# Third pair's preparation, the homes of the streamed factors and the order of masks in a fused routing-attention and feed-forward kernel

## The chip, the cores and the metric

The kernel runs on one core of one Trainium2 chip. A core has five engines with a queue of instructions each: TensorE (PE in the profile, with PEld for its weight loads), VectorE (DVE), ScalarE (ACT), GpSimd (POOL) and SyncE (SP), which here only issues transfers. The metric is the device time of one execution in microseconds (us); a kernel's time is the median of several executions.

## The reference

Attention with routing, then a feed-forward block. A query sees a key only if both fall to the same of 16 cluster centroids of their head.

```python
q_n, k_n, c_n = (t / (norm(t) + 1e-06) for t in (q, k, centroids))
q_assign = argmax(einsum('bhsd,hcd->bhsc', q_n, c_n), axis=-1)
k_assign = argmax(einsum('bhsd,hcd->bhsc', k_n, c_n), axis=-1)
mask = q_assign[:, :, :, None] == k_assign[:, :, None, :]
scores = where(mask, matmul(q, k.T) / sqrt(D), -1e9)
attn = softmax(scores)                      # (B, H, S, S)
x = matmul(attn, v)  ->  (B * S, H * D)
h = x @ w_in
out = (h - tanh(h)) @ w_out
```

The sizes are B = 4 batches, H = 8 heads, S = 768 positions, D = 64, a model width of 512 and an inner width of 2048. Inputs come as 64-bit floats, which the kernel reads as pairs of 32-bit words or rounds by itself; all matmuls are 32-bit.

## The kernel before

**Pairs, halves and steps.** Heads are taken in pairs: pair n is batch n // 4, heads 2p and 2p + 1 with p = n % 4; there are 16 pairs. A pair's 768 queries are two halves of 384, and its 768 keys are taken in three steps of 2 x 128. So one step is (pair, half, key step). The list `steps` starts with the first halves of pairs 0 to 3 (steps 0 to 11), goes on with their second halves (12 to 23), and then takes each later pair as a whole, six steps each (24 to 95). The number of a step is `at` in the code. `HP` is 4, `HALF` is 12, `NS` is 3, `HF` is 8, `CH` is 2.

**Work of one pair before its steps.** `load` fetches q, k and v (192 KB per head and input). `turn` transposes q and k so that D lies on the partitions: for pairs 0 to 3 by PE through a PSUM tile of the pool `ps_s` and a copy by ScalarE or VectorE. `similar` multiplies with the centroids into a PSUM tile of `ps_f`, `turn_back`, `route` and `route_on` find the cluster of each position on VectorE, `publish` writes the clusters of the queries as codes to DRAM, and `spread` reads them back, laid out to all partitions as a row (`row`); for the first half of pairs 1 to 3, `spread_both` fetches them into a tile `hot` instead, and `one_hot` makes from it two factors which PE adds to the scores, so that these steps need no mask on VectorE.

**Work of one step.** `begin` multiplies keys and queries (line 502, `sc`; with the factors of `hot`, line 513) and takes the exponential on ScalarE (line 524). `select` masks one of the step's two tiles on VectorE (line 534, two instructions, one for each head); after the second one GpSimd adds the tiles to a running sum (lines 546 and 550). `value` multiplies with v (line 559, `av`). The sums over keys are made by PE: in the first halves of pairs 0 to 3 in each step (`sum_up`, line 574, `den`), later from GpSimd's sums (`total_both`, line 620). In a turn of the step loop, PE is given the scores of the next step, the values of the current one, and then pieces of the feed-forward block as a fill; `todo` is the list of the other engines' work, the masks of the next step first, which is dealt out between the pieces of the fill (`between`).

**PSUM.** Scores and transposes share `ps_s` with two tiles; similarities, sums and the products of the feed-forward block share `ps_f` with three.

**The feed-forward block.** The first half of batch 0 is computed plainly (lines 733 and 749, steps 12 to 23). From step 24 on the products are made by a seven-product (Strassen-like) scheme: `up_product` (line 936, `pu`) for `x @ w_in`, `down_product` (line 1041, `pd`) for the second matmul. Its factors of w_in and w_out are sums of quarters, made once on VectorE (`up_maker` in steps 20 to 22, `down_maker` from step 36 on), kept in DRAM (`up_factors`, `down_factors`) and streamed back, 896 KB or 1024 KB at a time, by `fetch_factors`; three such tiles are held at once. `up_maker(0)` works on `w_in[0]` and `w_in[2]`, `up_maker(1)` on `w_in[1]` and `w_in[3]`. A streamed tile is asked for when product 6 of two before is made. `right_factors` makes differences of columns of x (`diff`, line 902), and the results of products are added on VectorE into `t`, `u`, `g` or `G` (line 931), which frees the PSUM tile. The plain and the first scheme's results go through tanh on ScalarE (line 990) and a subtraction on GpSimd (line 991).

**Weights.** w_in and w_out come in 32 pieces of 512 KB, which GpSimd asks for (`fetch`, three ahead), ScalarE works on twice (`rest_of`, lines 150 and 151) and VectorE twice (`round_piece`, lines 159 and 162); `paces` says how many in each step.

**What sets the order.** The kernel is emitted under a manual schedule: each engine runs its instructions in the order in which the code emits them, and waits on semaphores in that order. A transfer on SP waits in SP's queue until what it needs is there, and what stands behind it on SP waits too. The opening, before the loop over steps, is written out by hand:

```python
        load(1)
        load(0, (2,))
        turn(0, 0, nc.scalar); turn(0, 1, nc.vector)
        similar(0); turn_back(0); keep_warm(2); route(0); route_on(0)
        turn(1, 0, nc.scalar); turn(1, 1, nc.scalar); keep_warm(3)
        publish(0); load(2, (0,)); spread(0, 0)
```

`keep_warm(n)` gives PE n matmuls whose result nobody reads. The work of the pairs 2 and later before their steps is put into steps by the table `ready`; for pair 2 its transposes lie in step 0, its similarities and routing in step 1.

Of the kernel before, what the change touches and what calls it, by code (L numbers as in the profile page):

```python
# [58 lines left out]
def kernel(  # L59
# [120 lines left out]
    def fast():  # L180
# [18 lines left out]
        first_in = ExitStack()  # L199
        wp_in = first_in.enter_context(tc.tile_pool(name="wp_in", bufs=1, side="right"))  # L200
# [646 lines left out]
        def fetch_factors(n: int):  # L847

            if n < (B - 1) * PER:
                i = n + HF if n < 0 else n % PER  # L850
                t = streams[n] = late_pools["stream"].tile([P, HF, HM], F32, name="stream")
                if i < HF:
                    t = streams[n] = t.rearrange("p a b -> p (a b)")[:, 0 : 7 * CH * P].rearrange(
                        "p (c k f) -> p c k f", k=7, c=CH
                    )
                nc.sync.dma_start(t, up_factors[i] if i < HF else down_factors[i - HF])

        late_pools, half_pools, diffs = {}, {}, {}
        mid = ExitStack()

        def open_stream():
            first_in.close()
            late_pools["stream"] = cx.enter_context(
                tc.tile_pool(name="stream_late", bufs=3, side="right", reuse_waits="tile")
            )
            half_pools["diff"] = mid.enter_context(
                tc.tile_pool(name="diff_mid", bufs=1, side="right", reuse_waits="tile")
            )
            for n in range(2):
                fetch_factors(n - HF)  # L870

        def open_late():
            first.close()
            mid.close()
            for name, bufs in (
                ("diff", 1), ("u", 2), ("s", 2), ("th", 2), ("g", 1), ("left", 1), ("du", 1),
                ("c", 4), ("raw", 2), ("den", 1),
# [10 lines left out]

        def right_factors(b: int, c: int):

            if c == 0:
                diffs[b] = (
                    late_pools["diff"].tile([P, 3, CH, TB], F32, name="diff")
                    if b else half_pools["diff"].tile([P, 3, CH, TB // 2], F32, name="diff")
                )
# [99 lines left out]
        def strassen_items(b: int):  # L995
# [21 lines left out]
            def down_product(k_: int, j: int, between, rows_=False):  # L1017
# [25 lines left out]
                if which == 1:  # L1043
                    us[j] = late_pools["du"].tile([P, 2, HM], F32, name=f"du{j}")
# [74 lines left out]
        for n in range(2, len(pairs)):  # L1119
# [5 lines left out]
            for i, stage in enumerate(before(n)):  # L1125
                if stage:
# [60 lines left out]
        nc.gpsimd.tensor_copy(out=gate, in_=raw_qk[0, 1][:, 0, 1, 0:1])  # L1187
        for i in range(AHEAD):
            fetch(i)
        load(1)  # L1190
        load(0, (2,))
        turn(0, 0, nc.scalar)
        turn(0, 1, nc.vector)
        similar(0)
        turn_back(0)
        keep_warm(2)
# [4 lines left out]
        keep_warm(3)  # L1201
        publish(0)
        load(2, (0,))
        spread(0, 0)
        rest_of(0)
        similar(1)
        turn_back(1)
        keep_warm(1)
        load(2, (1,))
        rest_of(1)  # L1210

        nc.gpsimd.tensor_copy(out=gate, in_=rows[0, 0][:, 0, 0, 0:1])
        round_piece(rounding.pop(0))
        route(1)
        route_on(1)
        begin(steps[0])
        round_piece(rounding.pop(0))
        begin(steps[1])
        publish(1)
        select(*steps[0][:2], 0)  # L1220
        spread_both(1)
        begin(steps[2])
# [14 lines left out]
        paces = dict(enumerate((0, 0, 1, 1, 1, 0, 2, 1, 2, 1, 1, 0, 3, 2, 2, 2, 2, 2, 2, 3, 2)))  # L1237
# [3 lines left out]
        for at, (n, half, s) in enumerate(steps):  # L1241
# [4 lines left out]
            if at == 2 * HALF - 1:  # L1246
                open_stream()
# [3 lines left out]
            if at == 2 * HALF - 4:  # L1251
                makers = [it for i in range(2) for it in up_maker(i)]
            if at == 2 * HALF:
# [47 lines left out]
            if not taken:  # L1301
# [4 lines left out]
            if summed(n, half):  # L1306
                if 0 in stages:
                    stages.pop(0)()
                sum_up(n, half, s)
# [69 lines left out]
            if makers and at in light:  # L1379
                share = -(-len(makers) // len(light))  # L1380
                todo += makers[:share]
# [260 lines left out]
```

## Time and profile before

| what | us |
|---|---|
| median of 8 executions | 952.66 |
| lowest and highest of them | 950.91, 954.02 |
| the profiled execution | 953.53 |
| its span, first to last instruction | 951.8 |
| PE idle in the span | 17.2 |
| opening: first scores, first values | 15.43, 21.94 |
| scores of step 3 (first of pair 1) | 29.79 |
| first scores of step 25, with the fill of step 24 behind them | 195.57 |
| plain second matmul of batch 0's second half begins | 280.87 |

A line of a timeline has the start, the length, the engine, the line of the kernel, the operation with its tiles (written <- read) and shapes, the number of instructions, and in brackets the engine's idle time before it with what ended it. PE's records come two to a matmul of 32-bit numbers, so "x8" in the opening is four matmuls of the kernel. SPq, ACTq and POOLq are the queues that issue transfers; a line of theirs says when a transfer was issued, not when it landed. The chain that ended last follows the execution back from its last instruction; its shares say what the span was spent on.

### The profile page before, as it was taken

The numbers are of one execution on the slowest core, as the hardware profiler recorded it, in microseconds if no ns is written. First come the engines' busy times: TensorE is split into PE (matmuls) and PEld (weight loads), VectorE is DVE, ScalarE is ACT, GpSimd is POOL, SyncE is SP. The second block draws the span as 40 slices with busy tenths as digits, with TensorE's granted clock in tenths as the row PEclk, the third lists the DMA queues.
The fourth block names the chain that finished last, engine by engine and source line by source line (L and its number), as shares of the span: only waits on it lengthen the run. The fifth ranks groups of instructions, "written<-read, shape, count | busy, mean of one in ns | idle before, by whom it ended". The sixth has DMA issues, their size and how long they took to land.

```text
span 951.8 us, 16937 instructions
## 1 busy us (share of the span) xinstructions
PE 934.6 (98%) x6568; PEld 467.0 (49%) x6568; DVE 594.1 (62%) x1127; ACT 293.3 (31%) x453; POOL 510.7 (54%) x364
## 2 busy tenths in 40 slices
PE   8999999999999999999999999999999999999997
PEld 5434443355553334444466664444456665445664
DVE  7658677976687688657746567767756348443011
ACT  5586554223432232333321112332331220222000
POOL 1026343455665555778685453867797343657500
PEclk9999999999999999999999999999999999999999
DMA  8766454982737645474665646457344222323331
GB/s 201 199 193 145 156 139 128 277 248 74 191 102 185 158 129 125 154 188 108 193 166 195 153 144 204 114 177 181 113 130 148 98 84 101 117 80 131 107 106 37
DMA packets 168456, 139.92 MB, mean 147 GB/s; under 512 B 118272, under 2 KB 146736, under 8 KB 165680
## 3 DMA queue, kind: packets, MB, share of 16 engines
q1 hardware_dynamic: 161984, 117.23, 44.6%
q0 software_dynamic: 6240, 21.50, 6.7%
q8 instruction: 54, 0.88, 0.4%
q14 instruction: 34, 0.28, 0.1%
q10 hardware_dynamic: 144, 0.03, 0.0%
HBM read 117.48 MB, written 21.24 MB: 146 GB/s over the span
## 4 chain that ended last, share of the span: by engine, by line
PE 90%; DVE 5%; DMA 2%; POOL 1%; issue 1%; ACT 1%; SPq 0%; DVEq 0%; ACTq 0%; POOLq 0%
PE pu L936 25%; PE pd L1041 21%; PE sc L502 13%; PE av L559 13%; PE o L749 8%; PE h L733 4%; PE sim L378 1%; DVE e L534 1%; DMA stream<-up_factors 1%; PE den L574 1%; PE den L620 1%; POOL sum L550 1%; PE den L593 1%; DVE den L710 1%; DMA again<-in_moe_w_out_dram 1%
## 5 line engine op out<-in xcount | busy, mean ns | idle before, releaser
L550 POOL TENSOR_TENSOR sum<-sum,e 128x768 f32<-128x768 f32 x112 | 207.2, 1850 | 90.8 <-DVE e L534 86.0
L534 DVE SCALAR_TENSOR_TENSOR e<-row,code,sc 128x384 f32<-128x384 bf16 x336 | 186.0, 607 | 74.0 <-ACT sc L524 52.7
L1041 PE MATMUL pd<-stream,G 128*64 128x256 f32 (+1 forms) x1728 | 191.6, 379 | 0.0
L524 ACT ACTIVATE sc<-sc 128x768 f32<-128x768 f32 x168 | 125.9, 789 | 190.2 <-PE sc L502 156.6
L936 PE MATMUL pu<-xT,stream 128*64 128x384 f32 (+1 forms) x1024 | 159.3, 447 | 2.0 <-DVE g L931 0.9
L1041 PEld LDWEIGHTS pd<-stream,G 128*64 128x64 f32 (+1 forms) x1728 | 130.5, 144 | 61.7 <-issue 6.3
L502 PE MATMUL sc<-t,t 64*128 64x384 f32 x768 | 148.9, 506 | 0.5 <-ACT e L524 0.5
L559 PE MATMUL av<-e,vals 128*64 128x384 f32 x768 | 145.2, 498 | 1.2 <-DVE e L534 1.2
L1005 POOL TENSOR_TENSOR G<-G,th 128x768 f32<-128x768 f32 (+1 forms) x51 | 87.2, 1726 | 67.8 <-ACT th L1003 67.6
L936 PE MATMUL pu<-diff,stream 128*64 128x384 f32 (+1 forms) x768 | 120.8, 447 | 2.0 <-DVE G L931 1.0
L936 PEld LDWEIGHTS pu<-xT,stream 128*64 128x64 f32 x1024 | 73.1, 137 | 76.3 <-issue 60.0
L502 PEld LDWEIGHTS sc<-t,t 64*128 64x128 f32 x768 | 66.8, 186 | 73.6 <-issue 37.3
L546 POOL TENSOR_TENSOR sum<-e 128x768 f32<-128x768 f32 x28 | 52.7, 1881 | 74.4 <-DVE e L534 62.2
L559 PEld LDWEIGHTS av<-e,vals 128*64 128x64 f32 x768 | 47.5, 136 | 83.2 <-issue 77.9
L1003 ACT ACTIVATE th<-G 128x768 f32<-128x768 f32 (+1 forms) x51 | 40.9, 806 | 148.9 <-DVE G L931 144.1
L749 PE MATMUL o<-w_out,g 128*64 128x512 f32 x384 | 85.8, 592 | 0.0
L936 PEld LDWEIGHTS pu<-diff,stream 128*64 128x64 f32 x768 | 54.3, 137 | 59.4 <-issue 48.1
L931 DVE TENSOR_TENSOR G<-pu,u 128x384 f32<-128x384 f32 x72 | 39.7, 552 | 27.0 <-PE pu L936 27.0
L749 PEld LDWEIGHTS o<-w_out,g 128*64 128x64 f32 x384 | 27.5, 137 | 50.5 <-issue 50.0
L1056 DVE SCALAR_TENSOR_TENSOR c<-pd,du 128x256 f32<-128x256 f32 x36 | 15.1, 420 | 49.1 <-PE pd L1041 49.1
L733 PE MATMUL h<-xT,w_in 128*64 128x384 f32 x256 | 42.8, 486 | 0.0
L1056 DVE SCALAR_TENSOR_TENSOR du<-pd,du 128x256 f32<-128x256 f32 x31 | 13.0, 420 | 45.6 <-PE pd L1041 45.2
(139 smaller groups left out, 844.2 us busy)
## 6 DMA issues: line engine op xcount, KB each, us to landing
stream<-up_factors SPq DMA_DIRECT2D x32, 896.0 KB
stream<-down_factors SPq DMA_DIRECT2D x21, 1024.0 KB
raw<-in_moe_w_in_dram POOLq DMA_DIRECT2D x16, 512.0 KB, 4.5
raw<-in_moe_w_out_dram POOLq DMA_DIRECT2D x16, 512.0 KB, 4.6
again<-in_moe_w_in_dram SPq DMA_DIRECT2D x32, 256.0 KB
again<-in_moe_w_out_dram SPq DMA_DIRECT2D x32, 256.0 KB
vals<-in_v_dram SPq DMA_DIRECT2D x32, 192.0 KB
row<-q_codes SPq DMA_DIRECT2D x29, 192.0 KB
```

Of the source, the lines that this page charges most:

```text
L502: nc.tensor.matmul(sc[i][:, h, 0:TB], lhsT=turned[n, 1][r].rearrange("p a n -> p (a n)")[:, j * P : (j + 1) * P], rhs=turned[n, 0][r, half ...
L524: nc.scalar.activation(out=out, in_=sc[i][:, :, 0:TB], func=ACT.Exp, scale=SCALE)
L534: nc.vector.scalar_tensor_tensor(out=e[:, h].rearrange("p (j n) -> p j n", n=P), in0=rows[n, half][:, h], scalar=(codes[n][:, h, 1, j : j ...
L546: nc.gpsimd.tensor_tensor(out=s, in0=pair[0], in1=pair[1], op=ALU.add)
L550: nc.gpsimd.tensor_tensor(out=s, in0=s, in1=pair[i], op=ALU.add)
L559: nc.tensor.matmul(avs[n, half][h * D : h * D + D], lhsT=vals[n][:, h, j], rhs=e[i][:, h], start=(j == 0), stop=(j == NCH - 1),)
L733: nc.tensor.matmul(h[r], lhsT=w_in[i][:, c, o * P : (o + 1) * P][:, r], rhs=xT[c][:, half], start=(c == 0), stop=(c == CD - 1),)
L749: nc.tensor.matmul(acc[sub][r], lhsT=gs[f % HF][:, f // HF, sub * P : (sub + 1) * P][:, r], rhs=w_out[f // FQ][:, f % FQ], start=(f == seq ...
L936: nc.tensor.matmul(ps[r], lhsT=streams[base + i][:, c, k_, r], rhs=right[c], start=(c == 0), stop=(c == CH - 1),)
L1003: nc.scalar.activation(out=th, in_=t, func=ACT.Tanh)
L1005: nc.gpsimd.tensor_tensor(out=t, in0=t, in1=th, op=ALU.subtract)
L1041: nc.tensor.matmul(out_, lhsT=w, rhs=x, start=(i == 0), stop=(i == HF - 1))
```

## The change

Three parts, and what goes with them.

**The opening.** All of pair 2's q and k is loaded before the codes of pair 0 are published. Its transposes and similarities move from steps 0 and 1 ahead of the first values; its routing stays in step 1. The scores of steps 0, 1 and 2 are begun one by one as soon as their inputs exist. Five of the six filler matmuls between the pairs are gone. The first three weight pieces are no longer asked for together: each waits, through a copy on GpSimd into `gate`, for another transfer (pair 2's k, pair 0's row, pair 1's hot tile). The two pieces that were rounded in the opening are rounded in steps 1 and 5, and in a step of the first halves that has transposes these go ahead of the pieces on ScalarE.

**The factors.** Streamed factors no longer have tiles of their own in a pool that is opened in step 23 when w_in's is closed; they land in w_in[0], w_in[2] and w_in[1] in turn. The first two are asked for in step 21, once the first half of the factors has been issued, not in step 23. The differences of batch 0 and the scheme's `du` lie in w_in[3].

**The masks.** In steps 24 to 35 both masks of the next step are put ahead of the fill; before, the second one stood in slot 1 of the fill. Only in the step after a routing (26 and 32) both stand in slot 1. And in step 72, as in step 48 before, nothing is dealt out in the first piece of the fill.

```diff
@@ streams
-                t = streams[n] = late_pools["stream"].tile([P, HF, HM], F32, name="stream")
+                t = w_in[(0, 2, 1)[(n + HF) % 3]].rearrange("p c f -> p (c f)")
                 if i < HF:
-                    t = streams[n] = t.rearrange("p a b -> p (a b)")[:, 0 : 7 * CH * P].rearrange(
-                        "p (c k f) -> p c k f", k=7, c=CH
-                    )
+                    t = t[:, 0 : 7 * CH * P].rearrange("p (c k f) -> p c k f", k=7, c=CH)
+                else:
+                    t = t[:, 0 : HF * HM].rearrange("p (a b) -> p a b", b=HM)
+                streams[n] = t
                 nc.sync.dma_start(t, up_factors[i] if i < HF else down_factors[i - HF])
...
-        def open_stream():
-            first_in.close()
...
-            for n in range(2):
-                fetch_factors(n - HF)
...
+        kept_ = w_in[3].rearrange("p c f -> p (c f)")
...
@@ the table of stages
-                if stage:
+                if stage and (n > 2 or i > 1):
@@ the opening
-        nc.gpsimd.tensor_copy(out=gate, in_=raw_qk[0, 1][:, 0, 1, 0:1])
-        for i in range(AHEAD):
-            fetch(i)
+        def held_back(x):
+            nc.gpsimd.tensor_copy(out=gate, in_=x)
+
         load(1)
         load(0, (2,))
+        load(2)
         turn(0, 0, nc.scalar)
         turn(0, 1, nc.vector)
+        held_back(raw_qk[2, 1][:, 0, 1, 0:1])
+        fetch(0)
         similar(0)
         turn_back(0)
-        keep_warm(2)
+        begin(steps[0])
         route(0)
         route_on(0)
         turn(1, 0, nc.scalar)
         turn(1, 1, nc.scalar)
-        keep_warm(3)
         publish(0)
-        load(2, (0,))
         spread(0, 0)
-        rest_of(0)
+        held_back(rows[0, 0][:, 0, 0, 0:1])
+        fetch(1)
         similar(1)
         turn_back(1)
-        keep_warm(1)
-        load(2, (1,))
-        rest_of(1)
-
-        nc.gpsimd.tensor_copy(out=gate, in_=rows[0, 0][:, 0, 0, 0:1])
-        round_piece(rounding.pop(0))
+        begin(steps[1])
         route(1)
         route_on(1)
-        begin(steps[0])
-        round_piece(rounding.pop(0))
-        begin(steps[1])
+        turn(2, 0, nc.scalar)
+        turn(2, 1, nc.scalar)
+        begin(steps[2])
         publish(1)
+        similar(2)
+        keep_warm(1)
+        spread_both(1)
+        held_back(hots[1][:, 0, 0, 0:1])
+        fetch(2)
         select(*steps[0][:2], 0)
-        spread_both(1)
-        begin(steps[2])
         load(1, (2,))
         load(3)
@@ the loop over steps
-        paces = dict(enumerate((0, 0, 1, 1, 1, 0, 2, 1, 2, 1, 1, 0, 3, 2, 2, 2, 2, 2, 2, 3, 2)))
+        paces = dict(enumerate((0, 1, 1, 1, 1, 1, 2, 1, 2, 1, 1, 0, 3, 2, 2, 2, 2, 2, 2, 3, 2)))
...
+            turns_first = summed(n, half) and 0 in stages and not taken
-            if not taken:
+            if not taken and not turns_first:
                 for piece in todays[:2]:
                     rest_of(piece)
...
                 if 0 in stages:
                     stages.pop(0)()
+                if turns_first:
+                    for piece in todays[:2]:
+                        rest_of(piece)
...
+                if at < 2 * HALF and len(makers) > half_made >= len(makers) - share:
+                    todo += [lambda n=n: fetch_factors(n - HF) for n in range(2)]
...
-            slots = max(sum(it[1] for it in now) - (at == 4 * HALF), 1)
+            quiet = at in fills and at >= 4 * HALF
+            slots = max(sum(it[1] for it in now) - quiet, 1)
...
-                for it in todo[: masks - 1]:
-                    it()
-                second, todo = todo[masks - 1], todo[masks:]
+                first_masks, todo = todo[:masks], todo[masks:]
+                if 2 not in ready.get(at - 1, {}):
+                    for it in first_masks:
+                        it()
+                    first_masks = []
...
-                if second and i == min(slots - 1, 1):
-                    second()
+                if i == 1:
+                    for it in first_masks:
+                        it()
```

## The prediction

> **What bounds the kernel now.** I read the busy table first, then the chain that ended last.
>
> ```profile
> PE 934.6 (98%) x6568; PEld 467.0 (49%) x6568; DVE 594.1 (62%) x1127; ACT 293.3 (31%) x453; POOL 510.7 (54%) x364
> ...
> PE 90%; DVE 5%; DMA 2%; POOL 1%; issue 1%; ACT 1%; SPq 0%; DVEq 0%; ACTq 0%; POOLq 0%
> ```
>
> TensorE (PE) is busy for 934.6 of 951.8 us, and the change takes only a few filler matmuls from it. So the gain can come from the 17 us in which PE stands still, from the fillers, and from nothing else; I looked for those places in the timeline of PE.
>
> ```profile
> 17.25 1.62 PE L502 MATMUL sc<-t,t 64*128 64x384 f32 x8 [0.27 <-ACT e L524]
> ...
> 21.94 2.45 PE L559 MATMUL av<-e,vals 128*64 128x384 f32 x8 [1.24 <-DVE e L534]
> 24.32 1.53 PE L357 MATMUL pt<-ident,x 128*128 128x128 f32 x12
> 25.77 0.85 PE L574 MATMUL den<-e,ones 128*32 128x384 f32 x8
> 26.78 0.86 PE L378 MATMUL sim<-t,bd 128*32 128x192 f32 x16 [0.15 <-ACT t L364]
> ...
> 39.84 0.86 PE L378 MATMUL sim<-t,bd 128*32 128x192 f32 x16 [0.45 <-ACT t L364]
> ...
> 200.46 1.52 PE L936 MATMUL pu<-xT,stream 128*64 128x192 f32 x16 [0.58 <-DMA stream<-up_factors]
> ...
> 214.99 0.87 PE L936 MATMUL pu<-diff,stream 128*64 128x192 f32 x8 [0.98 <-DVE t L931]
> ...
> 233.32 0.84 PE L620 MATMUL den<-sum,ones 128*32 128x384 f32 x4 [1.39 <-POOL sum L550]
> ...
> 250.78 0.87 PE L936 MATMUL pu<-xT,stream 128*64 128x192 f32 x8 [0.88 <-DVE g L931]
> ...
> 273.87 0.84 PE L620 MATMUL den<-sum,ones 128*32 128x384 f32 x4 [0.62 <-POOL sum L550]
> ...
> 589.30 1.51 PE L936 MATMUL pu<-diff,stream 128*64 128x384 f32 x8 [1.04 <-DVE G L931]
> ```
>
> The number in brackets is PE's idle time just before the group. Three places matter: the opening, steps 24 to 35 (198 to 280 us), and step 72. From 40 to 198 us no gap stands in that list, so what the opening gains is kept. The other queues show what the gaps wait for:
>
> ```profile
> 16.93 0.48 SPq L457 DMA_DIRECT2D row<-q_codes  x1
> ...
> 22.85 1.16 SPq L466 DMA_DIRECT2D hot<-q_codes  x2
> ...
> 181.90 0.86 SPq L457 DMA_DIRECT2D row<-q_codes  x1
> ```
>
> ```profile
> 21.25 6.46 DVE L534 SCALAR_TENSOR_TENSOR e<-row,code,e 128x384 f32<-128x384 bf16 x12 [0.81 <-DMA row<-q_codes]
> 29.80 0.42 DVE L477 TENSOR_SCALAR hot<-hot,mine_code 128x768 bf16<-128x768 bf16 x1 [2.10 <-DMA hot<-q_codes]
> ```
>
> Each line has the start, the length, the engine and the line: SP asks for pair 0's row of codes and pair 1's hot tile, and VectorE (DVE) waits for both to land.
>
> **Opening.** Before, the codes of pair 0 reach SP at 13.93, the row is asked for at 16.93, and its twelve masks start at 21.25. Only then does PE do pair 2's transposes (1.45 us), its similarities (0.79) and sum 0 (0.78) between the values. After, pair 2's transposes and similarities and the scores of steps 0 to 2 stand ahead of the first values, in place of six filler matmuls, of which one stays.
> PE up to the first values: pair 0's similarities end at 10.41, as before. Scores and transposes share two PSUM buffers, so PE and ScalarE alternate. By the rows (half a score pair or of a pair's transposes 0.75, half an exponential or copy 0.75, with 0.05 between): scores, exponentials, transposes, copies of pair 1 to 14.25; similarities 14.7; scores of step 1 to 16.2; pair 2's copies to 18.55; scores of step 2 to 19.3; similarities and a filler to 20.45.
> Row: SP issues pair 2's four loads before the codes now, so the row needs only the codes' round trip (20.47 to 22.85 at the next one, 2.38): 13.93 + 2.38 = 16.31. Issue to first mask took 4.32 before (16.93 to 21.25). Bounds for it: 4.32, and 2.36, the codes' own transfer in the chain. Fewer weights are in flight (the three 512 KB loads are held back by gates), the size is the same: I take 3.7, near the row's own. Masks start at 20.0.
> Four masks cost 2.15 us (6.46/12 each), so the second values' last operand is ready 4.3 us after the start, its last matmul 0.36 later, sum 1 0.78 later: scores of step 3 start 5.45 us after the row, at 25.45. Before they start at 29.86, 8.6 after it. Gain 4.4; 3.15 if the row is no earlier; 4.9 if PE sets it (20.45 and twice 1.44 + 0.78).
> Next late: pair 1's hot tile. Issue to use was 6.95 (22.85 to 29.80). Pair 1's routing starts at 14.75 and, without the two weight pieces between, takes 3.3: codes 18.1, hot asked for at 20.5, ready at 27.45, and 0.65 for the two hot operations, 28.1; PE wants it at 26.94. That is a wait of 1.2 at worst and of none if it lands 1.2 sooner, as with one 512 KB load in front instead of two (1.05 MB at the 129 to 379 GB/s of the windows around 23 us is 3 to 8 us). I take 0.4: the opening gives 4.0, between 1.5 and 4.9.
> The dropped weight pieces return at steps 1 and 5, 1.4 us of ScalarE and 1.1 of VectorE each; a step is 4.04 and ScalarE's other work in it at most 2.5, so PE hides them. At step 3 the copies go ahead of the pieces, and the 0.45 at 39.84 goes.
> The fillers keep the clock up. The first fourteen records of them took 0.35 each (4.92/14) and six later ones 0.24, but the granted clock is 1.00 in every stretch of the opening, and no gap that I work out is over 1 us. The Trainium skill, TensorE: Matmul & The Clock Gate, section What's actually happening, speaks against dropping them: after an idle window of some 3.4 us the array runs at half clock for as long. By that rule a row some 3 us later than I think would cost about 1.7 us more (an estimate from that page); by the rows it costs nothing.
>
> **Early factors.** Two loads of 896 KB are issued in step 21, ahead of pair 4's row, instead of with a third in step 23. The 0.58 at 200.46 goes. But the row is queued behind them: 1.835 MB at 331 GB/s (the window 190 to 200) is 5.5 us. Before, the row was issued at 181.90 and used at 187.03, with VectorE waiting for ScalarE, not for it. Landing after 4.32 as in the opening, at 186.2, it now comes at 191.7: VectorE 4.7 late at worst.
> ```profile
> 187.03 2.19 DVE L534 SCALAR_TENSOR_TENSOR e<-row,code,sc 128x384 f32<-128x384 bf16 x4 [0.27 <-ACT sc L524]
> ...
> 197.41 1.14 DVE L534 SCALAR_TENSOR_TENSOR e<-row,code,sc 128x384 f32<-128x384 bf16 x2 [0.20 <-ACT sc L524]
> ...
> 199.99 0.36 DVE L931 TENSOR_TENSOR g<-pu,t 128x192 f32<-128x192 f32 x1 [1.44 <-PE pu L936]
> ```
> Behind these masks wait two transposes, reciprocals and differences (187.03 to 197.2 in all), then four masks instead of two (2.2), then the first g: 201.9 + 2.2 + 0.3 = 204.4. PE, freed of the 0.58, wants that PSUM buffer for its fifth product at 201.0 and got it at 201.78 before: 2.6 us later than before at worst, 0.8 sooner if the row overtakes the loads. I take 1.5 lost, nearer the late end, as the row and the loads share SP's queue. The third load and the differences in w_in[3] come behind the last products, which move back by the same 5.5 us, and are wanted after 200.
> A rule beside it: DMA: Bandwidth & Descriptors, section Queues, rings and completion order, says that each DMA engine takes one queue's descriptors in ring order. With it the whole 5.5 us stands; without it the term would be the 0.8 gained.
>
> **Masks first.** In ten of steps 24 to 35 both masks of the next step now go ahead of the products; in 26 and 32, behind a routing, they go later. 214.99: at step 26 the mask (1.13) stood ahead of the two t; now t goes first, 0.98 gone. 233.32 and 273.87: GpSimd adds the last e, whose second mask ended at 228.3; with both first it ends at 226.7 and the two adds (3.71) at 230.5, before the matmul's 231.9: 1.39 and 0.62 gone. 250.78: g stood behind the second mask (1.04) and a transpose: 0.88 gone. Sum 3.87. Against it: a step's first result leaves PSUM up to 1.13 later. Step 28, whose scores start at 222.62: masks 224.53 to 226.7, first product done at 226.1, and PE needs its buffer again three products of 0.65 later, 228.1: no wait. I take 3.5, bounds 0 and 3.87.
>
> **Step 72.** The first G goes ahead of two masks (1.05), 1.04 gone, and the next scores may wait 0.25 for the masks: 0.8, bounds 0.5 and 1.04. That du and differences lie in w_in[3] costs nothing: same instructions, same waits on PE.
>
> **Sum.** 4.0 + 0.45 - 1.5 + 3.5 + 0.8 = 7.25. The profiled execution took 953.53 (span 951.8), 0.87 above the median 952.66: 952.66 - 7.25 = 945.4.
>
> **Rivals.**
> One: masks first bring waits of their own and the stretch gives nothing: 952.66 - 4.0 - 0.45 + 1.5 - 0.8 = 948.9. For it: VectorE is 62% busy. Against: the 2 us of slack at step 28.
> Two: the opening is bound by transfers anyway, giving 1.5: 947.9. For it: the DMA share is 0.98 in the first 10 us. Against: less is in flight.
> Three: the row is not held up and PE sets the opening: 4.9 + 0.45 + 0.8 + 3.87 + 1.04 = 11.1, 941.6.
> Four, the slower side: in each of the ten steps PE waits the whole second mask, 10 x 1.13 = 11.3: 948.9 + 11.3 = 960.2. It decides from 0.37 us a step on (3.75 gained elsewhere). It needs ScalarE's exponentials some 2 us later in each step than at step 28.
>
> **Numbers.** Forecast 0.56, rival one 0.16, two 0.10, three 0.10, four 0.08. Under 0.2% (1.9 us, about what a measurement of this kernel can tell from no change) would count as the same: 0.05, out of rivals one, two and four; slower 0.06; faster 0.89. Range 941.0 to 950.0: rival three below, one and two with 1 us more above.
>
> **What would show it.** Right: step 3's scores near 25.4 instead of 29.8; no gap over 0.3 at the four places in steps 26 to 35; a VectorE wait for the row near 187 less the 4.4 already gained, and PE waiting some 2 us at the fifth product. Wrong: a row that lands no sooner than 21, a hot wait of PE over 1 us, or new gaps before pu in most steps of the stretch.

## The result and the profile after

The changed kernel takes 956.48 us (median of 21 executions, 951.62 to 959.65); the kernel before, on the same chip, 952.89 (59 executions). The ratio is 1.0033 with a 95% interval of 1.0025 to 1.0042: 0.33% slower, where 945.4, some 0.8% faster, was forecast. The changed kernel's executions spread over 8 us, those of the kernel before over 3.5, and their granted clocks run from 0.998 (the one of 952.48) to 0.991 (that of 959.65), which fits stalls that cost more in some executions than in others. The profiled execution took 956.18, its span 954.3. First the page of the changed kernel, its busy table and the shares of the chain that ended last:

```profile
PE 935.8 (98%) x6558; PEld 466.3 (49%) x6558; DVE 592.1 (62%) x1127; ACT 292.9 (31%) x453; POOL 514.3 (54%) x365
...
PE 90%; DVE 5%; DMA 3%; issue 1%; ACT 0%; SPq 0%; POOL 0%; DVEq 0%; POOLq 0%
```

These hardly differ from before. Where the time went is seen by following one event through the program: the start of the scores of each step. The columns are that time before, and how much later (+) or sooner (-) it came in the profiled execution of the changed kernel and of six experiments told below (from the traces' start times; one execution each).

| step | before, us | after | late loads (e1) | row first (e2) | routed first (e5) | piece moved (e9) | masks alone (e4) | both repairs (e7) |
|---|---|---|---|---|---|---|---|---|
| 3 | 29.79 | -2.13 | -3.35 | -3.51 | -3.36 | -3.45 | -0.56 | -3.70 |
| 9 | 56.79 | -2.42 | -3.31 | -3.81 | -3.24 | -3.74 | -0.56 | -3.63 |
| 13 | 73.41 | +4.70 | +3.58 | +1.91 | -3.25 | -3.74 | -0.56 | -3.63 |
| 25 | 195.57 | +5.10 | +3.58 | +1.91 | -3.24 | -2.15 | -0.56 | -3.63 |
| 27 | 209.06 | +9.35 | +4.01 | +1.66 | +1.95 | +2.49 | -0.64 | -3.49 |
| 37 | 278.04 | +4.19 | -1.16 | -3.51 | -3.22 | -2.40 | -5.82 | -8.68 |
| 74 | 590.75 | +2.72 | -2.64 | -4.24 | -4.57 | -3.87 | -5.85 | -10.14 |

Read the column "after" downwards: the opening gains 2.42; between steps 9 and 13 nearly three times that is lost (+7.12); between 25 and 27 another 4.25 go; the masks bring 5.16 back by step 37, and step 72 another 1.47. So two places lose, and both are stalls of PE in its timeline:

```profile
22.28 2.45 PE L558 MATMUL av<-e,vals 128*64 128x384 f32 x8 [0.56 <-DVE e L533]
...
27.66 1.56 PE L501 MATMUL sc<-t,t 64*128 64x384 f32 x8
...
59.78 0.82 PE L512 MATMUL sc<-hot 64*128 64x384 bf16 x4 [3.86 <-DVE hot L480]
60.54 2.83 PE L558 MATMUL av<-e,vals 128*64 128x384 f32 x8
63.30 1.51 PE L573 MATMUL den<-e,ones 128*32 128x384 f32 x8
64.73 2.16 PE L501 MATMUL sc<-t,t 64*128 64x384 f32 x8
...
69.38 0.85 PE L573 MATMUL den<-e,ones 128*32 128x384 f32 x8
70.17 1.56 PE L501 MATMUL sc<-t,t 64*128 64x384 f32 x8
...
209.63 1.55 PE L925 MATMUL pu<-w_in,w_in 128*64 128x192 f32 x8 [3.35 <-DVE g L920]
211.11 2.36 PE L501 MATMUL sc<-t,t 64*128 64x384 f32 x8
...
239.66 0.85 PE L619 MATMUL den<-sum,ones 128*32 128x384 f32 x8
...
592.07 1.46 PE L925 MATMUL pu<-diff,w_in 128*64 128x384 f32 x8
```

At step 9 PE waits 3.86 us for pair 3's hot tile, and what follows the wait is slow: the same eight records of scores take 2.16 at 64.73 and 1.56 at 70.17, those of sums 1.51 and 0.85. The fifth product waits 3.35 for g. The last two lines answer to the old gaps at 233.32 and 589.30: the same groups, with nothing in brackets. VectorE shows what stands behind the two waits:

```profile
21.61 6.44 DVE L533 SCALAR_TENSOR_TENSOR e<-row,code,e 128x384 f32<-128x384 bf16 x12 [2.94 <-ACT e L523]
...
59.08 0.42 DVE L476 TENSOR_SCALAR hot<-hot,mine_code 128x768 bf16<-128x768 bf16 x1 [5.86 <-DMA hot<-q_codes]
...
197.01 2.19 DVE L533 SCALAR_TENSOR_TENSOR e<-row,code,sc 128x384 f32<-128x384 bf16 x4 [4.08 <-DMA row<-q_codes]
...
209.22 0.62 DVE L920 TENSOR_TENSOR g<-pu,t 128x192 f32<-128x192 f32 x2
```

Both are waits for a transfer on SP's queue, whose issues in the changed kernel are these:

```profile
47.62 0.58 SPq L436 DMA_DIRECT2D q_codes<-qc  x1
51.48 1.11 SPq L465 DMA_DIRECT2D hot<-q_codes  x2
...
187.51 1.53 SPq L856 DMA_DIRECT2D w_in<-up_factors  x2
189.08 1.35 SPq L456 DMA_DIRECT2D row<-q_codes  x1
```

The hot tile is asked for at 51.48 and used at 59.08, 7.60 later. In the kernel before these were 50.55 and 55.52, 4.97 apart, and PE came to the factors only at 58.18, 2.0 us after the second operation on the tile (55.85 and 0.31) had ended. SP, VectorE and PE of the kernel before:

```profile
50.55 1.11 SPq L466 DMA_DIRECT2D hot<-q_codes  x2
```

```profile
55.52 0.42 DVE L477 TENSOR_SCALAR hot<-hot,mine_code 128x768 bf16<-128x768 bf16 x1 [0.21 <-DMA hot<-q_codes]
55.85 0.31 DVE L481 TENSOR_SCALAR hot<-hot,mine_code 128x384 bf16<-128x384 bf16 x1
```

```profile
58.18 0.49 PE L513 MATMUL sc<-hot 64*128 64x384 bf16 x4
```

What else was in flight is told by GpSimd's issues of weight loads, 512 KB each: first the kernel before, then the changed one.

```profile
46.31 0.53 POOL L219 DMA_DIRECT2D raw<-in_moe_w_in_dram  x1 [7.03 <-DVE w_in L159]
53.63 0.53 POOL L219 DMA_DIRECT2D raw<-in_moe_w_in_dram  x1 [6.80 <-ACT rest L151]
```

```profile
46.60 0.53 POOL L218 DMA_DIRECT2D raw<-in_moe_w_in_dram  x1 [7.11 <-ACT xT L583]
48.34 0.76 POOL L218 DMA_DIRECT2D raw<-in_moe_w_in_dram  x1 [1.21 <-DVE w_in L159]
51.20 0.53 POOL L218 DMA_DIRECT2D raw<-in_moe_w_in_dram  x1 [2.11 <-DMA raw<-in_moe_w_in_dram]
52.80 0.53 POOL L218 DMA_DIRECT2D raw<-in_moe_w_in_dram  x1 [1.06 <-ACT rest L151]
```

Before, nothing is asked for between 46.31 and 53.63; after, three loads are, and the hot tile's transfer lies among them. Each weight piece that is rounded frees a buffer, and GpSimd asks for the next 512 KB. The load at 48.34 comes from the piece that the change put into step 5; those at 51.20 and 52.80 belong to step 6, as those from 53.63 on did before, and come 2.4 and 2.2 us sooner with the step. Last the clock, in the stretches around the two stalls of the changed kernel (columns: window, its length, busy time of PE, PEld, DVE, ACT, POOL with instructions, granted clock, DMA share, GB/s):

```profile
60.00:70.00 10.00, 10.00 (x52) 3.04 (x48) 5.01 (x11) 7.12 (x12) 2.62 (x4) 0.70 0.47 129
...
210.00:220.00 10.00, 10.00 (x82) 5.43 (x80) 5.55 (x13) 2.03 (x3) 6.45 (x5) 0.86 0.39 64
```

Before, the granted clock was 1.00 at 60 to 70 us:

```profile
60.00:70.00 10.00, 10.00 (x72) 3.71 (x72) 7.47 (x13) 8.80 (x15) 3.91 (x5) 1.00 0.66 177
```

### The profile page after: what moved, and what is told of

Its sections match the earlier page's. It is cut to its first block, busy times and chain, and to the rows that moved or that the text cites. A ratio compares the mean times of both kernels' runs of the same rounds, so it can differ in the third digit from the quotient of the medians.

```text
span 954.3 us, 16920 instructions
## 1 busy us (share of the span) xinstructions
PE 935.8 (98%) x6558; PEld 466.3 (49%) x6558; DVE 592.1 (62%) x1127; ACT 292.9 (31%) x453; POOL 514.3 (54%) x365
## 4 chain that ended last, share of the span: by engine, by line
PE 90%; DVE 5%; DMA 3%; issue 1%; ACT 0%; SPq 0%; POOL 0%; DVEq 0%; POOLq 0%
PE pu L925 27%; PE pd L1030 23%; PE sc L501 13%; PE av L558 13%; PE o L748 6%; PE h L732 4%; DMA hot<-q_codes 2%; PE sim L377 1%; DMA row<-q_codes 1%; DVE made L833 1%; PE den L619 1%; DVE e L533 1%; DMA q_codes<-qc 1%; PE den L592 1%; DVE den L709 1%
## 5 line engine op out<-in xcount | busy, mean ns | idle before, releaser
L1030 PE MATMUL pd<-w_in,G 128*64 128x256 f32 (+1 forms) x1728 | 191.6, 379 | 0.0
L1030 PEld LDWEIGHTS pd<-w_in,G 128*64 128x64 f32 (+1 forms) x1728 | 130.5, 144 | 61.7 <-issue 6.1
L925 PE MATMUL pu<-xT,w_in 128*64 128x384 f32 (+1 forms) x1024 | 158.7, 447 | 0.6 <-PE pu L925 0.4
L501 PE MATMUL sc<-t,t 64*128 64x384 f32 x768 | 150.9, 511 | 0.5 <-ACT t L363 0.2
L925 PEld LDWEIGHTS pu<-xT,w_in 128*64 128x64 f32 x1024 | 73.2, 137 | 74.2 <-issue 60.4
L925 PE MATMUL pu<-diff,w_in 128*64 128x384 f32 x576 | 101.6, 487 | 0.0
L925 PEld LDWEIGHTS pu<-diff,w_in 128*64 128x64 f32 x576 | 41.0, 137 | 51.7 <-issue 45.4
L1047 DVE SCALAR_TENSOR_TENSOR c<-pd,w_in 128x256 f32<-128x256 f32 x36 | 15.1, 420 | 48.9 <-PE pd L1030 48.9
L1047 DVE SCALAR_TENSOR_TENSOR w_in<-pd,w_in 128x256 f32<-128x256 f32 x31 | 13.0, 419 | 44.3 <-PE pd L1030 43.8
```

The lines of the kernel that those rows point to most:

```text
L501: nc.tensor.matmul(sc[i][:, h, 0:TB], lhsT=turned[n, 1][r].rearrange("p a n -> p (a n)")[:, j * P : (j + 1) * P], rhs=turned[n, 0][r, half ...
L925: nc.tensor.matmul(ps[r], lhsT=streams[base + i][:, c, k_, r], rhs=right[c], start=(c == 0), stop=(c == CH - 1),)
L1030: nc.tensor.matmul(out_, lhsT=w, rhs=x, start=(i == 0), stop=(i == HF - 1))
```

## The experiments

Theory: the change is slower because of two transfers that came late (pair 3's hot tile, pair 4's row), each followed by a slow clock; opening, masks and step 72 bring gains, as was forecast.

**The factor loads at their old place (e1), and behind the row (e2).** The diff is that of e1, at the head of step 23; in e2 the same three lines stand in step 22 (`2 * HALF - 2`), behind the `spread` of pair 4's row, and the same two lines go.

```diff
+            if at == 2 * HALF - 1:
+                for m in range(2):
+                    fetch_factors(m - HF)
...
-                if at < 2 * HALF and len(makers) > half_made >= len(makers) - share:
-                    todo += [lambda n=n: fetch_factors(n - HF) for n in range(2)]
```

> The changed kernel, but the first two factor loads are issued at the head of step 23 again, behind all products and behind pair 4's row. Theory (the row waits in SP's queue behind 1.8 MB of factors, so VectorE starts pair 4's masks 4.9 us late and everything behind them): VectorE's wait for the row in front of these masks (4.08 us in the changed kernel) falls under 0.5, PE's wait of 3.35 us before its fifth product goes, the 0.6 us wait for the factors returns; 956.5 - 4.25 + 0.6 = about 952.9. Rival (PE waits because all four masks now stand ahead of the first g): the row is early but PE still waits 2 us or more before the fifth product; 955 or more.

> The changed kernel, but the two early factor loads are issued in step 22, one transfer later: right behind pair 4's row instead of right in front of it. Theory (only the place against the row matters): the masks of pair 4 start without a wait for the row, PE's waits of 3.35 and 0.6 us both go; about 952.2. Rival (the two loads cost whatever their place, since they push the last products of the factors and with them VectorE's makers back): the masks or the makers wait 2 us or more; 955 or more.

Measured: e1 951.11 us, ratio 0.9979 (0.9966 to 0.9992); e2 950.87, 0.9979 (0.9967 to 0.9991). Either takes 5.1 us from the changed kernel ((1.0033 - 0.9979) x 952.9). VectorE and PE of e2:

```profile
190.79 2.19 DVE L533 SCALAR_TENSOR_TENSOR e<-row,code,sc 128x384 f32<-128x384 bf16 x4 [0.54 <-DMA row<-q_codes]
```

```profile
203.41 0.87 PE L925 MATMUL pu<-w_in,w_in 128*64 128x192 f32 x8 [0.32 <-DVE g L920]
```

The wait for the row falls from 4.08 to 0.54, that of PE from 3.35 to 0.32, and the product behind it takes 0.87 again instead of 1.55. In e1 the fifth product does not wait, and the old gap for the factors is back at 0.82. So it is the order of row and loads on SP, not the place of the factors in w_in. The hot tile's stall stays in both (5.24 and 3.91 of PE's time).

**Weight pieces of steps 5 to 7 later (e3).**

```diff
-        paces = dict(enumerate((0, 1, 1, 1, 1, 1, 2, 1, 2, 1, 1, 0, 3, 2, 2, 2, 2, 2, 2, 3, 2)))
+        paces = dict(enumerate((0, 1, 1, 1, 1, 0, 0, 0, 2, 2, 2, 2, 3, 2, 2, 2, 2, 2, 2, 3, 2)))
```

> The changed kernel with the weight pieces of steps 5, 6 and 7 rounded (and so the next ones asked for) in steps 8 to 11 instead. Theory one (pair 3's hot tile is late because 512 KB weight pieces share the DMA engines with it): its time from issue to use falls from 7.6 us to about 5, PE's wait of 3.86 us falls under 1.5 and the slow clock behind it goes; about 950. Rival (it is late because its codes are late, VectorE routing pair 3 only behind pair 2's hot tile): codes still at 47 us, hot tile asked for at 50 or later, PE's wait still 2.5 us or more; 954 or more.

Measured: 956.63 us, ratio 1.0045 (1.0031 to 1.0060): no gain. The hot tile's stall did go: with no load asked for between 45.17 and 59.95, the tile, asked for at 49.54, was used at 53.73, 4.19 later. But the pieces now stood ahead of the masks on VectorE, four steps on, and waited there for their own loads. VectorE and PE of e3:

```profile
69.15 0.43 DVE L159 TENSOR_SCALAR w_in<-raw 128x512 uint32<-128x512 uint32 x1 [1.29 <-DMA raw<-in_moe_w_in_dram]
...
74.80 2.18 DVE L533 SCALAR_TENSOR_TENSOR e<-row,code,sc 128x384 f32<-128x384 bf16 x4
```

```profile
76.08 2.93 PE L501 MATMUL sc<-t,t 64*128 64x384 f32 x8 [5.70 <-DVE e L533]
```

The stall was moved and not removed: 5.70 at step 13 instead of 3.86 at step 9.

**Only the piece of step 5 moved on (e9).** It undoes one of the two pieces (steps 1 and 5) which the change adds in that line and which the forecast had costed at nothing.

```diff
-        paces = dict(enumerate((0, 1, 1, 1, 1, 1, 2, 1, 2, 1, 1, 0, 3, 2, 2, 2, 2, 2, 2, 3, 2)))
+        paces = dict(enumerate((0, 1, 1, 1, 1, 0, 2, 1, 2, 1, 1, 1, 3, 2, 2, 2, 2, 2, 2, 3, 2)))
```

> The changed kernel with the weight piece that it put into step 5 moved on to step 11, so that step 5 takes none, as before. Theory (half of the hot tile's delay is transfers: with the piece, four weight loads are asked for between 46.6 and 52.8 us against one before 53 us in the kernel before, and the hot tile takes 7.0 us against 4.4): pair 3's hot tile lands some 5 us after its issue, PE's wait in step 9 falls from 3.9 to 1 to 2.5 us, the clock stays over 0.9, and the time is 3 to 4.5 us less than the changed kernel's: 952 to 953.5. Rival (only the late request counts, because VectorE routes pair 3 behind its wait for pair 2's hot tile): the wait stays at 3.5 us or more and the time at 955.5 or more.

Measured: 950.43 us, ratio 0.9982 (0.9971 to 0.9994), 4.9 us less than the changed kernel and below the theory's range. In its profile the wait is not shortened but gone. SP and VectorE of e9:

```profile
49.02 1.11 SPq L465 DMA_DIRECT2D hot<-q_codes  x2
```

```profile
53.59 0.42 DVE L476 TENSOR_SCALAR hot<-hot,mine_code 128x768 bf16<-128x768 bf16 x1 [2.03 <-DMA hot<-q_codes]
```

Asked for at 49.02, used at 53.59: 4.57. The late request alone, the rival, is refuted: e2 asked at 49.58 and used the tile at 57.75. The gain is not kept whole, though: the table shows 1.59 lost again between steps 13 and 25, most of it in a new wait at step 13.

```profile
76.96 6.03 PE L732 MATMUL h<-xT,w_in 128*64 128x384 f32 x36 [1.44 <-DVE xT L712]
```

The piece that now belongs to step 11 stands on VectorE ahead of the reciprocals of the sums that PE waits for: these start at 73.74, in e5, where no piece stands there, at 72.64.

**Pair 3 routed ahead of pair 2's hot tile (e5).** In step 4 VectorE waits for pair 2's hot tile (42.19) and only behind it routes pair 3, so pair 3's codes reach SP only at 47.62 (45.15 to 46.41 in the other experiments on the changed kernel that keep this order).

```diff
-            todo += [stages[i] for i in (5, 3, 4) if i in stages]
+            first_of = (3, 4) if at == 4 else (5, 3, 4)
+            todo += [stages[i] for i in first_of if i in stages]
             route_items = stages.get(2, [])
             todo += route_items if isinstance(route_items, list) else [route_items]
+            if at == 4:
+                todo.append(stages[5])
```

> The changed kernel, but in step 4 VectorE routes pair 3 before the two operations on pair 2's hot tile, for which it waits. Theory two (the codes are late because routing stands behind that wait): pair 3's codes reach SP near 44.5 instead of 47.6, the hot tile is asked for near 48 instead of 51.5, PE's wait of 3.86 us falls under 1 and the slow clock behind it goes; about 949.5. Rival (weight pieces on the DMA engines): the tile is asked for sooner but takes longer, PE still waits 2 us or more.

Measured: 948.64 us (four executions), ratio 0.9956 (0.9939 to 0.9972), 7.3 less than the changed kernel. VectorE of e5, at the hot tile and at the row:

```profile
53.02 0.42 DVE L476 TENSOR_SCALAR hot<-hot,mine_code 128x768 bf16<-128x768 bf16 x1 [0.96 <-DMA hot<-q_codes]
...
189.44 2.19 DVE L533 SCALAR_TENSOR_TENSOR e<-row,code,sc 128x384 f32<-128x384 bf16 x4 [4.11 <-DMA row<-q_codes]
```

The tile still travels 5.96 us among the loads (asked for at 47.06), but was asked for early enough, and the gain of the opening arrives whole at step 25 (-3.24). The other stall is untouched, so the two are independent.

**Fillers in the wait of step 9 (e6).** This separates the idle time from the slow clock.

```diff
+            if step == steps[9]:
+                keep_warm(14)
             for i in parts:
```

> The changed kernel with fourteen filler matmuls (128x256, into a PSUM buffer that nothing reads) between the scores and the hot matmuls of step 9, where PE otherwise stands idle for 3.9 us. Theory (part of the stall's cost is the clock that the idle time brings): the hot tile comes no sooner, but the values, tallies and scores behind it take 1.5, 0.85 and 1.56 again instead of 2.83, 1.51 and 2.16, the granted clock of 60 to 70 us is over 0.9 instead of 0.70, and the time is 2 to 3 us less than the changed kernel's: about 954. Rival (the slow matmuls come from something else, say the loads in flight): they stay long, and the time is 956.5 or, with fillers that run past the hot tile, up to 1 us more.

Measured: 954.17 us, ratio 1.0018 (1.0009 to 1.0028), some 1.4 less than the changed kernel, under the 2 to 3 expected. PE of e6 (26 of the 28 records of the fillers lie in the stretch shown), then its window:

```profile
54.83 5.78 PE L303 MATMUL warm<-inverses 128*128 128x256 f32 x26
60.53 0.50 PE L514 MATMUL sc<-hot 64*128 64x384 bf16 x4
60.96 1.51 PE L560 MATMUL av<-e,vals 128*64 128x384 f32 x8
62.40 0.85 PE L575 MATMUL den<-e,ones 128*32 128x384 f32 x8
63.19 1.56 PE L501 MATMUL sc<-t,t 64*128 64x384 f32 x8
```

```profile
60.00:70.00 10.00, 10.00 (x69) 3.73 (x69) 5.23 (x11) 7.90 (x13) 2.37 (x4) 1.00 0.65 169
```

The granted clock is 1.00 instead of 0.70, and the four groups behind the wait take 4.42 instead of 7.32: the slow clock alone cost 2.9 us. The time shows less because the fillers ran too long. The tile was ready at 57.76 here, and PE came out of them at 60.53.

**The masks alone, on the kernel before (e4).**

```diff
-                for it in todo[: masks - 1]:
-                    it()
-                second, todo = todo[masks - 1], todo[masks:]
+                first_masks, todo = todo[:masks], todo[masks:]
+                if 2 not in ready.get(at - 1, {}):
+                    for it in first_masks:
+                        it()
+                    first_masks = []
...
-                if second and i == min(slots - 1, 1):
-                    second()
+                if i == 1:
+                    for it in first_masks:
+                        it()
```

> The kernel before, with only the order of the masks in steps 24 to 35 changed as in the changed kernel. Theory (the masks' term was right in kind; in the changed kernel the stretch from step 28 to 37 gained 5.2 us): the four gaps of 0.98, 1.39, 0.88 and 0.62 go and no other stands in their place, 3.9 to 5.2 us less, near 948.5. Rival (the stretch gained only because the changed kernel came to it 8 us later, so that VectorE and GpSimd had caught up): under 1.5 us less, 951.5 or more, with gaps left before pu or den.

Measured: 947.58 us, ratio 0.9944 (0.9928 to 0.9959): 5.3 us gained by this part alone, a little over the expected, and the scores of step 37 come 5.18 sooner against those of step 27. PE of e4, where the sums waited 1.39 before:

```profile
228.23 1.51 PE L559 MATMUL av<-e,vals 128*64 128x384 f32 x8
229.67 0.85 PE L620 MATMUL den<-sum,ones 128*32 128x384 f32 x8
```

**Step 72 alone, on the kernel before (e8).**

```diff
-            slots = max(sum(it[1] for it in now) - (at == 4 * HALF), 1)
+            quiet = at in fills and at >= 4 * HALF
+            slots = max(sum(it[1] for it in now) - quiet, 1)
...
-                it[2](between if i or at != 4 * HALF else lambda: None)
+                it[2](between if i or not quiet else lambda: None)
```

> The kernel before, with only the first product of later fills left without work between (at step 72 the first G goes ahead of two masks). Theory: the 1.04 before pu at 589 us goes, and scores of step 74 start 1.0 to 1.5 us sooner: 951.2 to 951.7, nothing else differs. Rival (the gain of 1.46 there came from elsewhere in the changed kernel, say the tiles in w_in[3]): within 0.3 us of before, with the gap in place or moved to the next scores.

Measured: 952.19 us, ratio 0.9995 (0.9986 to 1.0004). The trace says theory: the gap is gone and the scores of step 74 come 1.46 sooner against those of step 73. The times can't tell it from nothing: 1.46 us would be a ratio of 0.9985, just outside the interval. As a gain in time it stays unproven.

**Both repairs (e7): e2 and e5 together.**

> The changed kernel with both repairs: the two factor loads behind the row in step 22, and pair 3 routed ahead of pair 2's hot tile in step 4. Theory (the two stalls are independent and each repair holds on its own): both gaps go, no granted clock under 0.95, and what is left of the gains adds up: 3.2 kept to step 25, 0 to 0.3 at the factors, 5.2 for the masks, 1.5 less 0.8 lost again between, so 8.5 to 9.5 less than before: 943.5 to 944.5. Rival (one stall hides behind the other, or a later one takes its place): the time stays at 947.5 or more, with a new gap of over 1 us before the masks or the products.

Measured: 943.25 us (four executions, 942.03 to 943.52), ratio 0.9894 (0.9879 to 0.9909): by the ratios 10.1 us below the kernel before and 13.2 below the changed one. That it lies 2 us from the 945.4 forecast for the change as it stands says little for that sum: here the opening gives 0.8 less, factors, masks and step 72 together 3.7 more than their terms. The table's last column shows every gain kept: 0.14 is lost from step 9 to 27, the masks bring 5.19, step 72 1.46. The one wait of PE over 0.3 us after the first 10 us is this:

```profile
198.27 0.87 PE L925 MATMUL pu<-w_in,w_in 128*64 128x192 f32 x8 [0.72 <-DVE g L920]
```

**The two mispriced steps undone, routing left as it is (e10): e2 and e9 together.**

> The changed kernel with the two steps undone that the forecast priced too low: step 5 takes no weight piece, and the two factor loads are asked for in step 22 behind pair 4's row; the order of routing is left as the change has it. Theory (these two account for the whole miss; opening, masks and step 72 are right): no gap at the hot tile nor at the fifth product, no granted clock under 0.95, offsets to before of about -3.5 to step 25, -3.5 at step 27, -8.5 at step 37, -10 at step 74: 942.5 to 944.5, as with both repairs before. Rival (routing pair 3 early is needed too once PE is 3.5 us ahead): a wait of over 1 us at the hot tile in step 9 in this run, and 946 or more.

Measured: 945.37 us, ratio 0.9916 (0.9902 to 0.9929). Theory and rival each have a part of the runs: five executions took 943.92 to 945.67, two 949.10 and 950.40, and the profiled one is the 949.10. In it the stall is there, and its granted clock and that of the execution of 950.40 are 0.997, where the other five have 0.999 to 1.000. GpSimd, SP, VectorE and PE of e10:

```profile
49.69 0.53 POOL L218 DMA_DIRECT2D raw<-in_moe_w_in_dram  x1 [3.96 <-ACT rest L151]
```

```profile
49.16 2.25 SPq L465 DMA_DIRECT2D hot<-q_codes  x2
```

```profile
57.00 0.42 DVE L476 TENSOR_SCALAR hot<-hot,mine_code 128x768 bf16<-128x768 bf16 x1 [5.64 <-DMA hot<-q_codes]
```

```profile
57.70 0.66 PE L512 MATMUL sc<-hot 64*128 64x384 bf16 x4 [3.30 <-DVE hot L480]
```

Up to here e10 is the same program as e9, where the next load was asked for 0.87 us behind the tile and the tile took 4.57. Here it was 0.53 behind, SP needed 2.25 instead of 1.11 to issue the tile, and it took 7.84. So moving the piece does not exclude the stall, though by times and clocks most executions seem free of it; asking for the tile 2 us earlier (e5, e7) took it away in both profiles, and in the four executions of e7 the times lie within 1.5 us.

## Why the prediction was wrong

**The step that failed.** "From 40 to 198 us no gap stands in that list, so what the opening gains is kept." No gap meant that the limit was near, not that there was none. In the kernel before, pair 3's hot factors were ready at 56.16 (55.85 and 0.31) and PE wanted them at 58.18: 2.0 us of slack, less than the gain of 4.4 that was forecast for PE. Its chain (hot tile of pair 2, routing, codes, hot tile) runs over VectorE and SP and moves less than PE: where the routing stands as the change has it, the tile was asked for between 0.9 us later (51.48) and 1.5 sooner (49.02, e9) than before, while PE came 2.4 to 4.0 sooner. A wait of up to 2.4 could have been worked out from such rows; the forecast watched pair 1's tile and stopped there.

**The same place, costed at nothing.** "The dropped weight pieces return at steps 1 and 5 [...] so PE hides them" counted 1.4 us of ScalarE and 1.1 of VectorE and left out the 512 KB load that each piece sets off. That load, and step 6's two that came 2.4 us sooner, fell into the hot tile's 5 us, which became 7.6. By the sum: forecast 0 from step 9 to 25, measured +7.52, of which 3.86 are idle time and 2.9 slow clock. Used-up slack and loads beside the tile are both needed: with no load near it (e3), or with the next two a little later (e9), the tile was ready 0.7 and 0.2 us before PE wanted it, and with the loads there but the tile asked for early (e5, e7) too; none of these four loses anything from step 9 to 12. In e10's profile, where the loads came close without the piece of step 5, 5.1 are lost at step 9.

**The row behind the loads**: right mechanism, too small. Forecast 1.5, between -0.8 and 2.6; measured 4.25 between steps 25 and 27 of the changed kernel; there e1 and e2 lose 3.8 and 4.5 less. The wait for the row was put at "4.7 late at worst" and is 4.08, and the 12.7 from the row's masks to the fifth product (191.7 to 204.4) were 12.6 (197.01 to 209.63). So the worst case of 2.6 held in size, with the clock on top: of the 4.25, 2.8 is idle time (3.35 less the 0.58 that went) and 1.5 the clock (0.80 on the scores at 211.11, 0.68 on the product before). Its parts did not: measured against PE the row was issued 2.1 us later than before (189.08 against 181.90, PE 5.10 later), and its way took 7.93, not 4.32 and 5.5. Taking less than the worst case had no row for it: the two issues stand 1.6 us apart in one queue. The rule that the forecast weighed there, the Trainium skill, DMA: Bandwidth & Descriptors, section Queues, rings and completion order (descriptors of one queue taken in ring order), was the better guide; the trace agrees, with 7.93 us from the row's issue to its use, against 6.17 in e2, where it stands ahead of the loads, and 5.13 at most before, when VectorE was not waiting for it.

**The clock.** "By the rows it costs nothing" held for the rows of before, whose longest gap in the stretches used was 1.39. The changed kernel has gaps of 3.35 and 3.86, and paid 1.5 and 2.9 us for them. The Trainium skill, TensorE: Matmul & The Clock Gate, section What's actually happening, has half clock after an idle window of about 3.4 us; the trace agrees on the half clock (granted 0.50 from 61 to 65 us; 1.51 for 0.85, 2.83 for 1.51), while shorter waits brought it too: 3.35 here, and 2.67 ahead of e6's fifth product, with 0.83 granted in the 10 us behind it. Of the ten waits of 2.67 to 5.70 us in these profiles, eight have 0.83 or 0.84 in the 10 us behind them, an estimated 1.6 to 1.7 us lost (ten times what is missing to 1), near the 1.7 that the forecast had worked out from that page. Those of 5.70 (e3) and of 3.86 have 0.76 and 0.69, but that of 5.24 (e1) has 0.84: the 2.9 is the dear end, and the length of a wait does not tell which it will be. The forecast had tied that rule to the opening only, where no such gap came.

**The opening**: forecast 4.45 with the copies of step 3, measured 2.42 in the profiled execution, but 3.10 to 3.99 at step 9 in the eight other profiles with the same opening (e1, e2, e3, e5, e6, e7, e9, e10). In these the row's masks start at 19.95 to 20.43, as the 20.0 of the working; in the changed kernel's own at 21.61. There the row itself was late, though the bracket of that line names ScalarE: GpSimd's copy that waits for the same row started at 21.23, in e7 at 19.57.

```profile
21.23 0.18 POOL L1180 CAST gate<-row 128x1 f32<-128x1 bf16 x1 [5.89 <-DMA row<-q_codes]
```

What was off in the others is PE: it is free for the first values at 21.64 in e7, not at 20.45, because the scores of step 2 run until 20.30 (19.3 forecast) and the similarities follow. So PE sets the end: 21.64 and twice 1.44 + 0.78 are 26.08, and the scores of step 3 start at 26.09 (25.45 forecast). In the changed kernel's own execution they start 6.05 after the masks, where the working has 5.45. Pair 1's hot tile cost PE 0.19 in e7, against 0.4 forecast. Rival two's 1.95 and rival three's 5.35 (with the 0.45 of step 3) lie outside all nine.

**Masks and step 72**: right, and larger. Forecast 3.5 and 0.8; measured 5.16 (5.18 alone, 5.19 in e7) and 1.47. The four gaps went as worked out, 3.87 in brackets, and no wait took their place, which refutes the first and the fourth rival. What they brought beyond the brackets is told at the end.

Together: -2.42 + 7.52 + 4.25 - 5.16 - 1.47 = +2.72 at step 74, where -7.25 was forecast. No rival named the place. The slower side was sought in VectorE's masks and came from two transfers on SP's queue.

## What to carry to other kernels

When an engine's work is moved forward, take each chain that meets it later on other engines, and write down its slack (ready against wanted) before calling the gain kept. A piece of work has the price of the transfers that it sets off as well: ask which small transfer with a reader waiting will lie beside or behind them, and put that one first. An idle time of some 3 us or more on TensorE cost its length here and, by the granted clock behind it, 1.6 to 3.1 us more.

## What the runs showed of the hardware

A small transfer's time depends on the bulk beside it, and on fractions of a microsecond. The hot tile (two of 192 KB) took from issue to use 4.19 with no load near (e3), 5.96 and 6.03 with one load 0.2 to 0.3 ahead of it (e5, e7), and 7.60 to 8.67 where two loads were asked for between 0.6 us ahead of it and 1.9 behind (after, e1, e2, e6, e10); where the two came 0.87 and 2.18 behind it (e9), it took 4.57. e10's executions at 944 and at 950 fit this; it was read from profiles and not tried by itself.

A gap of PE costs more than its bracket. Between steps 26 and 37 the gaps of the kernel before sum to 4.00 us and those of e4 to 0.17, yet e4 is 5.19 faster there (75.49 against 70.30); at step 72 a gap of 1.04 cost 1.47. That is some 0.3 to 0.4 for each gap, with the granted clock at 1.00 in both. At step 72 the rows account for it. In e8, without the wait, the next product starts at 587.97, 0.17 before the modelled end of the group of 32 records ahead of it (582.81 and 5.33). In the kernel before, with the wait, this group takes 5.53 (582.73 to 588.26), 0.20 more, the bracket counts only from their end, and the product behind takes 1.51 instead of 1.46: 0.17 + 0.20 + 0.05 = 0.42, the difference of 1.46 and 1.04. So the bracket, which counts from a modelled end, reads short; the other gaps were not taken apart like this.
